# The 32nd largest score of a row, found from the larger and the smaller ones of key pairs

## The chip, the core and the metric

The kernel runs on one core of one Trainium2 chip. A core has five engines with instruction queues of their own: PE (TensorE, matrix products and transposes), DVE (VectorE), ACT (ScalarE), POOL (GpSimd) and SP (SyncE, which here only issues DMAs). They work side by side and meet at semaphores. SBUF is the working memory of 128 partitions, PSUM holds what PE writes. The metric is the device time of one execution in microseconds; less is better. A profiled execution records every instruction on that core.

## The reference

Eight batches of eight heads; each head has 576 queries and 576 keys of 64 numbers. For each query the 32 highest scores are kept, the rest is masked, and the softmax of what is left weighs the values. The result goes through a Fourier mixing layer and a two-layer MLP.

```python
scores = scale * np.matmul(q, k.transpose(0, 1, 3, 2))
kth = np.partition(scores, -top_k, axis=-1)[..., -top_k:-top_k + 1]      # top_k = 32
mask = scores >= kth
scores = np.where(mask, scores, -1000000000.0)
scores = scores - np.max(scores, axis=-1, keepdims=True)
attn = np.exp(scores)
attn = attn / (np.sum(attn, axis=-1, keepdims=True) + 1e-09)
attn_out = np.matmul(attn, v)
...
mixed = np.real(fft(fft(x, axis=1), axis=2))                   # x: [8, 576, 512], heads side by side
u = x + mixed
un = (u - mean) / np.sqrt(var + 1e-06)
out = u + np.maximum(un @ w_ch1, 0.0) @ w_ch2                  # 512 -> 2048 -> 512
```

Two numbers per row of scores are needed from the selection: the maximum and the 32nd largest.

## The kernel before

The kernel is one long unrolled program, written out by hand in the order in which each engine gets its instructions. Two heads form a *pair*; 32 pairs make up the eight batches, four to a batch. The 576 queries of a head are cut into four tiles of 128 rows and a tail of 64. A pair has nine *items*: four tiles for each of its two heads (`e` is 0 or 1), and one item that holds the tails of both heads (`e` is `None`). So there are 288 items of 128 rows by 576 scores, 36 to a batch. In the order of a pair, items 0, 1, 2 and 3 are tiles, item 4 is the tails, items 5 to 8 are tiles.

The main loop (from L1589) goes over steps `i`; step `i` issues, among much else:

- on PE the scores of items `i + 3` and `i + 4` if item `i + 3` has `e == 0` (`scores`, L355): two products of 512 keys into two PSUM banks of the pool `ps_s`, which has two, and one product for the last 64 keys ("tails") of both. ACT copies each into an SBUF tile `S` of 576 columns (L425, L396). The 512 keys stand in columns 0 to 511 for `e == 0` with the tails behind them, and in columns 64 to 575 for `e == 1` with the tails in front;
- on DVE the selection (`top_ops`, L428): eight largest of a row (MAX8, L446), strike these out (MATCH_REPLACE8 with a MATCH_VALUE_LOAD, L448), and again; four maxima and three strikes of 576 columns an item. Step `i` has rounds 2 and 3 of item `i` and rounds 0 and 1 of item `i + 1`, interleaved one by one (L1704). Round 0 reads `S` and writes the struck row into a work tile `wk`;
- on POOL `bounds` (L451): the first and the 32nd of the 32 maxima, scaled, into `nt`; later `mask` (L466): ACT forms a penalty from `S` and `nt` (L469), POOL subtracts it (L472);
- on ACT `expo` (L476, its instruction is L480), the exponential of an item a step or two later.

Then the masked weights must be transposed. In the first batch, in pair 7 and in the last pair PE does that (`transposes`, L532). For all others (`by_dma`) ACT copies the two 16-bit halves of each number apart into `wk` (`plane`, L487), SP writes them to DRAM (L506) and reads them back transposed two or more steps later (`turn`, L515). `wk` is then free for another item; there are three such tiles for pairs of items and one for tails. PE multiplies the transposed weights by the values (`attend`, L576), in the first batch in pieces in the step behind the item, later four or five steps behind it.

The Fourier mixing and the MLP of a batch run in the steps of the next batch: PE's work for them is cut into units that a planner by expected PE costs (`fixed_cost`, `level`) spreads evenly over the steps, and which are put between the steps' other PE work. Since the last batch has no next one, its MLP runs alone at the end. In the first batch the MLP's weights are converted instead, on ACT, POOL and DVE (L209 to L238), and `centre` subtracts means from them.

Each engine takes its instructions in order, so one that waits holds all behind it.

Of the kernel before, what the change touches and what calls it, by code (L numbers as in the profile page):

```python
# [16 lines left out]
TOPK = 32  # L17
# [69 lines left out]
def kernel(  # L87
# [9 lines left out]
    nc = tc.nc  # L97
    B, H, S, D = q.shape
# [21 lines left out]

    fs_np, fd_np, sg_np, turn_np, rows_np = _tables(S, DM)
    fs_d = nc.inline_tensor(fs_np, name="c_fs")
    fd_d = nc.inline_tensor(fd_np, name="c_fd")
    sg_d = nc.inline_tensor(sg_np, name="c_sg")
    turn_d = nc.inline_tensor(turn_np, name="c_turn")
    rows_d = nc.inline_tensor(rows_np, name="c_rows")
# [116 lines left out]
    nat, qT_of, kT_of, v_of, PT, Ssb, Wk, Wp, M8, Nt = ({} for _ in range(10))  # L243
# [111 lines left out]
    def scores(i, part):  # L355
# [26 lines left out]
        if part == 1:  # L382

            copy = nc.scalar.copy if i else nc.vector.tensor_copy
            shape, name = [P, NF * P], f"sp_{i}_t"
            if by_dma(i):
                sp = ps_t.tile(shape, F32, name=name, tag="tp")
            else:
                sp = ps_s.tile(shape, F32, name=name, tag="sp") if i else bank(shape, name)

            q_end = P * t + rows
            nc.tensor.matmul(  # L392
                sp[:, 0:P], lhsT=qT[:, q_end - P:q_end], rhs=kt_t, start=True, stop=True
            )
            for h, (s_t, r, _, tails) in enumerate(to):
                copy(out=s_t[r, tails], in_=sp[P - rows:P, TAIL * h:TAIL * (h + 1)])  # L396
            return 0.3
# [21 lines left out]
        for h, (s_t, r, keys, _) in enumerate(to):  # L419
            hd = slice(D * h, D * (h + 1))  # L420
            sp = ps_s.tile([P, NF * P], F32, name=f"sp_{i}_{h}", tag="sp")
            nc.tensor.matmul(  # L422
# [5 lines left out]
    def top_ops(i, rounds):  # L428

        if not 0 <= i < N:  # L430
            return []
        if i not in Wk:
            e = items[i][2]
            if e != 1:

                if e is None:
                    Wp[i] = attp.tile([P, 1, S], F32, name=f"wk_{i}", tag="W1", bufs=1)
                else:
                    Wp[i] = attp.tile([P, 2, S], F32, name=f"wk_{i}", tag="W", bufs=3)
            Wk[i] = Wp[i - 1][:, 1, :] if e == 1 else Wp[i][:, 0, :]  # L440
            M8[i] = small.tile([P, TOPK], F32, name=f"m8_{i}", tag="m8", bufs=5)
        w, m, s = Wk[i], M8[i], Ssb[i]
        ops = []
        for r in rounds:
            src, m8 = s if r == 0 else w, m[:, 8 * r:8 * r + 8]
            ops.append(lambda src=src, m8=m8: nc.vector.max(out=m8, in_=src))  # L446
            if r < TOPK // 8 - 1:
                ops.append(lambda src=src, m8=m8: nc.vector.match_replace(w, m8, src, NEG))  # L448
        return ops

    def bounds(i):  # L451

        if i < N:
            Nt[i] = small.tile([P, 2], F32, name=f"nt_{i}", tag="nt", bufs=6)
            nc.gpsimd.tensor_tensor(  # L455
                out=Nt[i], in0=M8.pop(i)[:, 0:TOPK:TOPK - 1], in1=cc, op=ALU.mult
            )

# [901 lines left out]
    nc.vector.memset(cc[:, 0:1], -1.0)  # L1360

# [30 lines left out]
    prep("q", 0, ((2, NF), (NF, NC)))  # L1392
    scores(2, 0)
# [192 lines left out]
    for op in top_ops(0, (0, 1)):  # L1586
        op()
    i, carry = 0, 0.0
    while i < N + 5 or plan or queue or sums:  # L1589
        now[0] = i  # L1590
        run(i, "begin")
# [112 lines left out]
        first, second = top_ops(i, (2, 3)), top_ops(i + 1, (0, 1))  # L1704
        for n in range(max(len(first), len(second))):
            for ops in (second, first):
                if n < len(ops):
                    ops[n]()
                if ops is first and n == len(first) - 1:
                    run(i, "shift")  # L1710
        if not first:
# [4 lines left out]
        some_sums(max(2.1 - planned, 0.0))  # L1716
        bounds(i)
# [50 lines left out]
```

## Time and profile before

| what | value |
|---|---|
| median of three runs | 1781.06 us (1779.12 to 1782.7) |
| profiled execution, its time | 1780.27 us |
| its span, first to last instruction | 1778.5 us |
| mean granted TensorE clock | 0.964 |
| PE, DVE, ACT, POOL busy | 92%, 87%, 72%, 51% of the span |
| selection on DVE: MAX8 of `wk`, MAX8 of `S` | 617.4 us in 864, 214.5 us in 288 |
| selection on DVE: MATCH_REPLACE8 of `wk`, of `S` | 424.8 us in 576, 212.5 us in 288 |
| mask on POOL (L472) | 407.6 us in 288 |
| bounds on POOL (L455) | 58.7 us in 288, the last at 1603.5 us |

The span leaves out what lies before the first and behind the last instruction, 1.8 us of the profiled execution's own time. Busy time is the union of an engine's instructions. A line of a group names engine, operation, output and input with their shapes, the number of instructions, their busy time in us, the mean length of one in ns, and the idle time just before them with what ended it. A line of the order of time starts with the start and the length in us. Instructions of one engine can overlap by a little in these records, so the distance from one start to the next tells better what one costs than its length does. The page's chain of work that ended last goes through PE for 48% of the span, DVE 16%, ACT 16%, POOL 14%.

### The profile page before, as it was taken

What the parts mean: (1) busy time and instruction counts of PE and PEld (TensorE: products, weight loads), DVE (VectorE), ACT (ScalarE), POOL (GpSimd) and SP (SyncE); (2) the same over time, 40 slices, a digit from 0 to 9 for tenths busy, and PEclk for the clock granted to TensorE, in tenths of its full rate; (3) what the DMA queues carried; (4) which work ended last, traced back from release to release, by engine and by line L of the source; (5) the groups of instructions that cost most, each with busy time, mean ns of one, the idle gap of its engine ahead of it and who ended that gap; (6) DMA issues with size and microseconds to landing.
All of it is one profiled execution on the core that took longest, in us unless ns stands there. A gap on an engine that the chain in (4) does not pass through costs nothing.

```text
span 1778.5 us, 26295 instructions
## 1 busy us (share of the span) xinstructions
PE 1632.1 (92%) x7830; PEld 1040.9 (59%) x7830; DVE 1552.5 (87%) x3319; ACT 1278.8 (72%) x3136; POOL 906.6 (51%) x1268
## 2 busy tenths in 40 slices
PE   5666689999898989999999999999999999999998
PEld 3444455464455755566555755576566755577777
DVE  7999989999999999998999999999999999863121
ACT  6888759887787878876888778877978787653200
POOL 4768846655634565354544665356535564333000
PEclk7778799999999999999999999999999999999999
DMA  5333126651457855586557856595558655643151
GB/s 156 115 102 117 32 81 163 185 152 50 119 145 196 222 131 135 136 233 161 135 136 200 212 133 140 152 240 145 152 132 222 182 135 128 172 114 101 36 180 60
DMA packets 492926, 255.28 MB, mean 144 GB/s; under 512 B 364528, under 2 KB 483056, under 8 KB 492784
## 3 DMA queue, kind: packets, MB, share of 16 engines
q1 hardware_dynamic: 489008, 243.80, 52.5%
q0 software_dynamic: 2816, 9.44, 1.6%
q8 instruction: 63, 1.03, 0.2%
q14 instruction: 79, 0.65, 0.1%
q10 hardware_dynamic: 960, 0.36, 0.1%
HBM read 99.79 MB, written 84.74 MB: 104 GB/s over the span
## 4 chain that ended last, share of the span: by engine, by line
PE 48%; DVE 16%; ACT 16%; POOL 14%; issue 5%; DMA 2%; POOLq 0%; SPq 0%; DVEq 0%; ACTq 0%
PE hp L1055 18%; DVE m L446 7%; DVE wk L448 6%; PE o L585 6%; PE cw L1254 5%; POOL wk L472 5%; PE cv L1254 4%; PE sp L422 4%; ACT wk L469 3%; POOL fold L696 3%; PE cp L1120 2%; ACT wk L493 2%; PE cp L1082 2%; ACT S L425 2%; PE sp_t L392 1%
## 5 line engine op out<-in xcount | busy, mean ns | idle before, releaser
L472 POOL TENSOR_TENSOR wk<-S,wk 128x576 f32<-128x576 f32 x288 | 407.6, 1415 | 418.1 <-ACT wk L469 417.2
L446 DVE MAX8 m<-wk 128x8 f32<-128x576 f32 x864 | 617.4, 741 | 0.1
L1055 PE MATMUL hp<-unT,w 128*128 128x256 f32 (+1 forms) x2048 | 529.6, 409 | 6.8 <-ACT hT L1059 6.0
L1055 PEld LDWEIGHTS hp<-unT,w 128*128 128x128 f32 x2048 | 378.0, 191 | 112.0 <-ACT hT L1059 11.4
L448 DVE MATCH_REPLACE8 wk<-m,wk 128x576 f32<-128x576 f32 x576 | 424.8, 737 | 0.0
L469 ACT ACTIVATE wk<-S,nt 128x576 f32<-128x576 f32 x288 | 224.3, 779 | 96.8 <-POOL nt L455 96.3
L493 ACT COPY wk<-S 128x576 uint16<-128x576 uint16 x468 | 290.2, 673 | 0.0
L446 DVE MAX8 m<-S 128x8 f32<-128x576 f32 x288 | 214.5, 745 | 11.6 <-ACT S L396 11.6
L480 ACT ACTIVATE S<-wk,nt 128x576 f32<-128x576 f32 x234 | 185.1, 791 | 46.7 <-POOL wk L472 45.4
L448 DVE MATCH_REPLACE8 wk<-m,S 128x576 f32<-128x576 f32 x288 | 212.5, 738 | 0.0
L1082 PE MATMUL cp<-w,hT 128*128 128x512 f32 x448 | 206.0, 598 | 0.0
L1059 ACT ACTIVATE hT<-hp 128x320 f32<-128x320 f32 (+1 forms) x256 | 104.1, 411 | 140.7 <-PE hp L1055 139.7
L585 PE MATMUL o<-PT,v 128*64 128x256 f32 (+3 forms) x1440 | 196.1, 417 | 5.6 <-DVE wk L448 2.1
L422 PE MATMUL sp<-kT,qT 64*128 64x512 f32 (+1 forms) x528 | 160.1, 668 | 6.7 <-ACT S L414 3.6
L585 PEld LDWEIGHTS o<-PT,v 128*64 128x64 f32 x1440 | 113.2, 154 | 84.1 <-issue 24.8
L425 ACT COPY S<-sp 128x512 f32<-128x512 f32 (+1 forms) x264 | 141.7, 589 | 26.2 <-PE sp L422 25.2
L455 POOL TENSOR_TENSOR nt<-m,cc 128x2 f32<-128x2 f32 x288 | 58.7, 204 | 166.9 <-DVE m L446 160.4
L1254 PE MATMUL cw<-w,hT 128*128 128x256 f32 x512 | 119.7, 383 | 9.1 <-ACT ct L1225 6.2
L1082 PEld LDWEIGHTS cp<-w,hT 128*128 128x128 f32 x448 | 81.3, 193 | 75.1 <-issue 74.7
L392 PEld LDWEIGHTS sp_t<-kt,qT 128*128 128x128 f32 x320 | 51.7, 195 | 111.4 <-issue 73.3
L1254 PEld LDWEIGHTS cw<-w,hT 128*128 128x128 f32 x512 | 94.5, 190 | 27.3 <-ACT ct L1225 8.4
L1254 PE MATMUL cv<-w,hT 128*128 128x256 f32 x432 | 100.4, 383 | 6.6 <-DMA w<-w_parts 2.8
(155 smaller groups left out, 2036.3 us busy)
## 6 DMA issues: line engine op xcount, KB each, us to landing
planes<-wk SPq DMA_DIRECT2D x208, 288.0 KB, 2.7
w<-w_parts SPq DMA_DIRECT2D x94, 512.0 KB, 4.7
space<-in_moe_w_ch_dram SPq DMA_DIRECT2D x32, 512.0 KB, 3.6
nat<-in_q_dram SPq DMA_DIRECT2D x128, 64.0 KB, 2.3
v<-in_v_dram SPq DMA_DIRECT2D x32, 256.0 KB, 3.4
nat<-in_k_dram SPq DMA_DIRECT2D x62, 128.0 KB, 2.8
planes<-wk SPq DMA_DIRECT2D x52, 144.0 KB, 2.7
w_parts<-w_t POOLq DMA_DIRECT2D x8, 512.0 KB, 4.0
```

Source lines behind the costliest of these rows:

```text
L422: nc.tensor.matmul(sp[r], lhsT=qT[hd, q_cols], rhs=kT[hd, :], start=True, stop=True)
L425: nc.scalar.copy(out=s_t[r, keys], in_=sp[r])
L446: ops.append(lambda src=src, m8=m8: nc.vector.max(out=m8, in_=src))
L448: ops.append(lambda src=src, m8=m8: nc.vector.match_replace(w, m8, src, NEG))
L469: nc.scalar.activation(out=w, in_=Ssb[i], func=AF.Relu, scale=-FAR, bias=Nt[i][:, 1:2])
L472: nc.gpsimd.tensor_tensor(out=w, in0=Ssb[i], in1=w, op=ALU.subtract)
L480: nc.scalar.activation(out=Ssb[i] if by_dma(i) else w, in_=w, func=AF.Exp, bias=Nt.pop(i)[:, 0:1], accum_out=den_t[pair % 3][:, c:c + 1],)
L493: nc.scalar.copy(out=words[:, half, :], in_=src[:, half, :])
L585: nc.tensor.matmul(o[D * e:D * (e + 1), c0:c1], lhsT=vv[:, e, c, :], rhs=pt[:, NF if c == NF else (NF + 1) * e + c, c0:c1], start=(c == 0) ...
L1055: nc.tensor.matmul(hp[:, 0:w], lhsT=w1[:, dt, P * it:P * (it + 1)], rhs=unT[:, dt, 0:w], start=(dt == 0), stop=(dt == NDT - 1),)
L1082: nc.tensor.matmul(cp, lhsT=hT[:, it, P * n:P * (n + 1)], rhs=w2[:, it, :], start=(it == 0), stop=(it == NIT - 1),)
L1254: nc.tensor.matmul(dst, lhsT=h()[a][:, kc, :], rhs=rhs_of(kc), start=start and kc == 0, stop=kc == NK - 1, skip_group_check=True,)
```

## The change

The 256 items that are tiles become *paired*; the 32 tails items keep the old way.

For a paired item the 512 keys are halved: score `j` of the first half and score `j` of the second form a pair. `split` takes the larger of each pair into `wk` columns 0 to 255 and the smaller into columns 320 to 575, two DVE instructions of 256 columns, which read the second half from PSUM (`sp_of` keeps the bank) and the first half from its copy in `S`. `tails_along` copies the item's 64 tail scores into columns 256 to 319 on POOL. The selection then runs over the first 320 columns, four maxima and three strikes. The maxima of ranks 1 to 8 are kept, those of ranks 9 to 24 are written over, ranks 25 to 32 are kept; the eight largest of the 256 smaller ones stand beside them, and a last maximum over these 16 numbers gives eight, the last of which is the 32nd largest of all. That holds if fewer than eight smaller ones are among the row's 32 largest. `bounds` therefore also forms the difference between this number and the eighth of the smaller ones (POOL, one column, four columns in turn), DVE keeps the least of these twice in each pair of heads (`least_over`), and near the end PE adds up the rows with a difference of zero or less (`count_rows`). All engines load that count after the whole computation, and if it is over zero they run a second, complete copy of the program, `forward(..., False)`, with the old selection.

The order changes with it. `split` and `tails_along` of an item with `e == 0` stand at the head of step `i` for item `i + 2`, while the first maximum of that item still stands in step `i + 1`. `split` of an item with `e == 1` stands behind the fourth selection instruction of step `i` for item `i + 3`. The score banks are held until the splits have read them. The three `wk` tiles are named in turn by hand. The tail scores of both heads go into the transposes' banks (`ps_t`) after the first batch, and into a bank of `ps_m` in it. The constant tables are made outside the two calls of `forward`.

```diff
+    found = pool.tile([P, 8], F32, name="found", tag="found")
+    over, again = found[:, 0:NOVER + 1], found[0:1, 7:8].bitcast(I32)
+    args = (tc, q, k, v, moe_w_ch1, moe_w_ch2, out, tables, over, again)
+    forward(*args, True)
+    rows = nc.values_load(again, min_val=0, max_val=P)
+    with tc.If(rows > 0):
+        forward(*args, False)
...
-            if by_dma(i):
+            if i >= PER_BATCH:
                 sp = ps_t.tile(shape, F32, name=name, tag="tp")
             else:
-                sp = ps_s.tile(shape, F32, name=name, tag="sp") if i else bank(shape, name)
+                sp = bank(shape, name)
...
+            if e is not None:
+                sp_of[i + h] = sp, keys
...
+    w_ring = [attp.tile([P, 2, S], F32, name=f"w_{n}", tag=f"ring{n}", bufs=1) for n in range(3)]
+    HALF = NF * P // 2
+    WON = HALF + TAIL
...
+    def split(i):
+
+        if not paired(i):
+            return
+        w, (sp, keys) = work(i), sp_of.pop(i)
+        near_half = Ssb[i][:, keys][:, 0:HALF]
+        for to, op in ((w[:, 0:HALF], ALU.max), (w[:, WON:S], ALU.min)):
+            nc.vector.tensor_tensor(out=to, in0=sp[:, HALF:2 * HALF], in1=near_half, op=op)
+
+    def tails_along(i):
+
+        if paired(i):
+            e = items[i][2]
+            tails = slice(0, TAIL) if e else slice(NF * P, S)
+            nc.gpsimd.tensor_copy(out=work(i)[:, HALF:WON], in_=Ssb[i][:, tails])
+
+    def top_ops(i, part):
...
+        won = w[:, 0:WON] if pairs else w
+
+        place = (0, 1, 1, 2) if pairs else (0, 1, 2, 3)
+
+        def best(r):
+            n, src = place[r], won if r or pairs else s
+            return lambda: nc.vector.max(out=m[:, 8 * n:8 * n + 8], in_=src)
+
+        def strike(r):
+            n, src = place[r], won if r or pairs else s
+            return lambda: nc.vector.match_replace(won, m[:, 8 * n:8 * n + 8], src, NEG)
+
+        if part == 0:
+            return [best(0), strike(0), best(1), strike(1)]
+        ops = [best(2), strike(2), best(3)]
+        if pairs:
+            ops.insert(0, lambda: nc.vector.max(out=m[:, 24:32], in_=w[:, WON:S]))
+            ops.append(lambda: nc.vector.max(out=m[:, 8:16], in_=m[:, 16:32]))
         return ops
...
+            if pairs:
+                r = i % PER_PAIR
+                n = (r - (r > 4)) % NOVER
+                nc.gpsimd.tensor_tensor(
+                    out=over[:, n:n + 1], in0=m[:, 15:16], in1=m[:, 31:32], op=ALU.subtract
+                )
+
+    def least_over():
+        nc.vector.tensor_reduce(
+            out=over[:, NOVER:], in_=over, op=ALU.min, axis=mybir.AxisListType.X
+        )
...
+    def count_rows():
+
+        got = bank([1, 1], "rows")
+        nc.tensor.matmul(got, lhsT=over[:, NOVER:], rhs=cc[:, 0:1], start=True, stop=True)
+        nc.vector.tensor_scalar(
+            out=again, in0=got, scalar1=-1.0, scalar2=None, op0=ALU.mult
+        )
+        return 0.2
+
+    if in_pairs:
+        for n in range(NPAIR):
+            at(PER_PAIR * n + NOVER, "least", least_over)
+            at(PER_PAIR * (n + 1), "least", least_over)
...
+        at(N + 4, "pe", count_rows)
...
         now[0] = i
+        if i + 2 < N and items[i + 2][2] == 0:
+            split(i + 2)
+        if i + 2 < N and by_dma(i + 2):
+            tails_along(i + 2)
...
-        first, second = top_ops(i, (2, 3)), top_ops(i + 1, (0, 1))
+        if i + 2 < N and not by_dma(i + 2):
+            tails_along(i + 2)
+        first, second = top_ops(i, 1), top_ops(i + 1, 0)
         for n in range(max(len(first), len(second))):
...
+            if n == 1 and i + 3 < N and items[i + 3][2] == 1:
+                split(i + 3)
```

## The prediction

> **What bounds the kernel now.** I read the page's busy times first, then the windows by stage, then the groups by form, and last the order of time in a steady step and in a step of the first batch. The busy shares say that two engines are nearly full.
>
> ```profile
> PE 1632.1 (92%) x7830; PEld 1040.9 (59%) x7830; DVE 1552.5 (87%) x3319; ACT 1278.8 (72%) x3136; POOL 906.6 (51%) x1268
> ```
>
> An average hides which of them ends last where, so the same by stage (length; then busy us and instructions of PE, weight loads, DVE, ACT, POOL; granted clock; DMA share; GB/s):
>
> ```profile
> 0.00:240.00 240.00, 155.70 (x765) 96.32 (x767) 228.68 (x485) 185.50 (x440) 166.75 (x178) 0.77 0.32 98
> 250.00:800.00 550.00, 514.13 (x2402) 308.42 (x2402) 532.83 (x1138) 438.92 (x1084) 304.75 (x436) 0.98 0.60 156
> 800.00:1550.00 750.00, 735.38 (x3545) 458.14 (x3549) 706.08 (x1512) 590.32 (x1443) 392.88 (x584) 1.00 0.65 163
> 1550.00:1778.00 228.00, 218.01 (x1057) 171.61 (x1052) 78.99 (x172) 58.13 (x153) 42.02 (x70) 1.00 0.34 101
> ```
>
> The reader is to see three regimes. In the first batch and its hand-over (its 36th bounds instruction stands at 215.2) DVE is full (95%, and 99% from 50 to 200) while PE has 84 us of holes. From 800 on PE is 98% busy and DVE 94%: PE has only 14.6 us of holes in 750. At the end PE works alone. From 250 to 800 PE has 35.9 us of holes. Is a busy PE at its rate? Matmul ends are modelled, so I read starts:
>
> ```profile
> 1133.71 6.63 PE L1055 MATMUL hp<-unT,w 128*128 128x320 f32 x24
> ```
>
> That is 0.276 us for each matmul, though its group's mean duration is 433 ns. Adding the start-to-start times of all groups of one batch (1122.68 to 1316.14, 193.5 us) gives about 189 us. So PE is truly full there, and no relief of DVE can give more than its holes.
>
> What DVE does, by form, and a stretch of DVE alone in order of time:
>
> ```profile
> L446 DVE MAX8 m<-wk 128x8 f32<-128x576 f32 x864 | 617.4, 741 | 0.1
> L448 DVE MATCH_REPLACE8 wk<-m,wk 128x576 f32<-128x576 f32 x576 | 424.8, 737 | 0.0
> ...
> L630 DVE TENSOR_TENSOR x<-tpx,rd 128x256 f32<-128x256 f32 x57 | 24.0, 421 | 49.9 <-PE tpx L626 42.1 <-DMA out_dram<-x,out_list 5.4 <-PE hp L1055 1.0
> ```
>
> ```profile
> 1130.60 0.74 DVE L446 MAX8 m<-S 128x8 f32<-128x576 f32 x1
> 1131.27 0.73 DVE L446 MAX8 m<-wk 128x8 f32<-128x576 f32 x1
> ...
> 1135.42 0.41 DVE L630 TENSOR_TENSOR x<-tpx,rd 128x256 f32<-128x256 f32 x1
> 1135.75 0.74 DVE L446 MAX8 m<-S 128x8 f32<-128x576 f32 x1
> ```
>
> A pass over 576 columns occupies DVE for 0.67 us start to start, not 0.74, and the seven passes of an item with their three value loads take 4.82 us (1130.60 to 1135.42). A 128x256 tensor_tensor with its input in PSUM takes 0.33.
>
> **DVE, per paired item.** 256 of the 288 items become paired. Removed: 4.82 us. Added: seven passes over 320 columns. The slope per column comes from the adds at L880: 690 ns at 512 columns, 415 at 256, 1.07 ns a column; 0.67 less 256 columns is 0.40, so 2.77 us. Bounds: 0.37 (in proportion to width) and 0.67 (a pass does not shrink). The maximum of the 256 smaller ones by the same slope: 0.33. Three value loads: 0.18. The two splits are L630's form: 0.33 each, 0.66 (0.27, the 64x128 form's duration, to 0.42, its full duration). The last maximum of 16 numbers: 0.16, nearest to the reciprocal of 4 columns (161 ns); 0.06 to 0.25, since it directly follows the maximum it reads. Sum 4.10, saving 0.72 an item: 184 us. The 64 small minima cost 0.17 each (the 5-column tensor_scalar, 172 ns), 11 us. Net 173 us of DVE's 1552, or 0.6 us a step over nine items. With each pass at 0.67 DVE would instead do 1.2 us more an item; the two tensor_tensor rows and the smaller batch-norm rows all shrink with width, so I give that end little weight.
>
> [...]
>
> **What of this reaches the end, by stage.**
>
> First batch. It takes 5.55 us a step (27 bounds instructions at L455 between 50 and 200). Per step DVE is busy 5.51, ACT 4.75, POOL 4.43. DVE falls to about 4.9. POOL gains a 128x64 copy (0.25, between the 128x4 copy's 190 ns and the 64x64 add's 314) and a one-column subtraction (0.19, the 5-column rows): 0.39 a step, to 4.82. So three engines meet at 4.8 to 4.9, and the most to gain is 36 steps of 0.64, 23 us. But a loop comes in between:
>
> ```profile
> 107.57 2.72 PE L585 MATMUL o<-PT,v 128*64 128x128 f32 x20
> ...
> 110.22 1.13 PE L422 MATMUL sp<-kT,qT 64*128 64x512 f32 x4
> ...
> 111.38 1.07 ACT L425 COPY S<-sp 128x512 f32<-128x512 f32 x2
> ...
> 111.99 0.74 DVE L446 MAX8 m<-S 128x8 f32<-128x576 f32 x1
> ```
>
> PE's scores stand behind the attend matmuls, which wait for the previous item's exp. The split needs these scores at the head of a DVE step one step sooner than the first maximum did: here the first copy ends at 111.9 and DVE's step starts at 111.99. The slack is nothing. From the end of the DVE step whose exp the attend needs, to the copy, is two steps, 11 us, plus 0.2 for the subtraction that now stands between bounds and mask on POOL. Attend precedes paired scores so in two places of each nine steps, which ties four steps of nine to 11.2 us a pair. The other five can fall by 0.5: 20 steps, 10 us, less eight times 0.2. I take -8 (bounds -23 and +8, the second if all steps are tied, rival 2).
>
> 250 to 1550. DVE gets 10% of slack and PE stays. PE's 50 us of holes are waits on ACT above all (transposes behind L396 7.1 us, xT 3.3, unT 3.3 and kT 2.6 between 250 and 800). ACT is late where bounds on POOL wait for DVE, so part goes. I take 15, three tenths (0 to 50; next late is ACT's own order). Behind a split that waits stand both items' maxima, and behind those bounds and mask, which nobody needs for four steps here. The splits hold the two score banks until the middle of the next DVE step; PE needs them two PE steps later, so this is hidden while DVE is no more than 3 us behind. The tail scores move to the transposes' banks in the two later pairs that don't go by DMA, and to a bank of their own in the first batch: 10 instructions of 0.2 us each, nothing. SP gets no new DMA. POOL's tails copy now stands ahead of the mask and the fold work and waits for ACT's copy of the tails, emitted one step earlier, and for the ring's buffer: in one pair of items of each nine, its previous planes transfer (1142.67 plus 2.7 to landing) lands at 1145.4, as the DVE step starts at 1145.39. It is covered by POOL's 45% of idle time; if ACT is later, DVE and POOL stand there (rival 2).
>
> 1550 to the end. Two us earlier at most for the last items; -2. The last 122 us, from 1656, are PE alone and stay.
>
> The end. Five engines load the count, compare and jump over the second forward. No row shows a load of a register or a jump. Below: 0, beside the 2.6 us landing of the last output, which each run waits for anyway. Above: two small transfers in sequence at 4.4 us, some 9, and I take +5, the middle. [...]
>
> Sum: 1780.27 - 8 - 15 - 2 + 5 = 1760. The profiled execution is 0.8 below the median of the three runs, 1781.06, so the two agree within 0.05%.
>
> **Rivals.** 1: PE's holes were all DVE's doing and the first batch reaches its floor: -23, -50, -2, +5, so 1710. For it: PE's share of the chain of waits is only 48%, DVE, ACT and POOL taking turns. Against: the holes are behind ACT.
>
> 2, slower: the early split becomes the bound. Place: the head of DVE's step and POOL's tails copy. In the first batch every pair of steps then costs the loop plus 0.45 us of new POOL work, 18 times, +8; per nine steps afterwards one stand of up to 2 us on the planes transfer that also holds masks and folds, 26 of them with a fifth on PE's path, +10; end +5 to +9. About 1805, and 1793 with half of it. It decides once the loop is longer than 11.1 us for two steps. For it: zero slack at 111.99 and 1145.39. Against: DVE has 1.2 us to lose in two steps before it is where it was.
>
> 3: the gain is off the path everywhere: first batch -3, middle -3, end +5: 1779, the same.
>
> 4: a row fails and everything runs again, about 3540. From the reference's inputs I counted how many of the smaller of each pair are among a row's 32 largest: 5 at most in all rows, and eight would be needed. Under 1 in 100.
>
> **How the numbers follow.** A measurement of this kernel tells 0.2% from nothing. Chances: the forecast 0.54 (its own range 1745 to 1772), rival 1 0.14, rival 3 0.08, rival 2 0.23, rival 4 0.01. Faster 0.69, same 0.08, slower 0.23. The range 1725 to 1793 leaves out the far half of rivals 1 and 2.
>
> **What would show it.** Passes of 0.40 us start to start; splits of 0.42 duration without long waits before them; DVE busy near 1380; the 36th bounds instruction near 207 rather than 215.2; PE idle from 250 to the end of attention about 35; the last bounds near 1580 rather than at 1603.5; under 9 us between the last DMA issue's landing and the end. I am wrong if DVE waits on S or on planes for more than 100 us in all, if passes do not shrink, or if PE's holes stay at 50.

## The result, and the profile after

The changed kernel takes 1796.06 us (1795.84 to 1798.32) against 1780.09 (1777.33 to 1782.7) for the kernel before, each the median of four runs: a ratio of 1.0093, 95% interval 1.0075 to 1.0111, so 0.9% slower. The forecast was 1760. The second, complete program never runs. The profiled execution takes 1795.85 us, its span is 1794.0, the mean granted clock 0.968 (0.964 before).

The page's busy times of the changed kernel:

```profile
PE 1637.0 (91%) x7832; PEld 1040.3 (58%) x7832; DVE 1387.2 (77%) x4410; ACT 1280.8 (71%) x3136; POOL 993.6 (55%) x1780
```

DVE lost 165 us of work, as planned, and the kernel became slower. The same by stage (stretch, length, then busy us and instructions of PE, weight loads, DVE, ACT, POOL; granted clock, DMA share, GB/s):

```profile
0.00:240.00 240.00, 152.81 (x772) 93.32 (x773) 205.54 (x631) 186.06 (x441) 176.62 (x248) 0.81 0.34 98
250.00:800.00 550.00, 510.64 (x2371) 304.26 (x2370) 467.26 (x1512) 434.60 (x1074) 331.12 (x613) 0.98 0.60 152
800.00:1550.00 750.00, 734.88 (x3520) 456.28 (x3519) 626.73 (x2033) 590.59 (x1440) 435.95 (x825) 1.00 0.63 161
```

PE's holes, which were to be filled, are 39.4 us from 250 to 800 (35.9 before) and 15.1 from 800 to 1550 (14.6). In the same 550 us PE issued 31 matmuls fewer, and 25 fewer in the 750. Where that builds up is seen from the bounds instructions on POOL, of which both kernels have one per item. Their starts in us:

| bounds instruction | before | after | difference |
|---|---|---|---|
| 36 | 226.6 | 225.5 | -1.1 |
| 72 | 419.1 | 424.0 | +4.9 |
| 144 | 807.1 | 819.0 | +11.9 |
| 216 | 1199.7 | 1210.4 | +10.7 |
| 287, the last | 1603.5 | 1615.9 | +12.4 |
| from the last one to the end of the span | 175.0 | 178.1 | +3.1 |

(They are counted from 0. The prediction's 36th bounds instruction is number 35 here: it starts at 214.6, 215.2 before, and 207 was forecast.) So the first batch gains one microsecond, the time to 1600 loses 13.5 and the end 3.

The DVE groups of the changed kernel by form (busy us, mean ns of one, idle time before them and what ended it):

```profile
L498 DVE MAX8 m<-w 128x8 f32<-128x320 f32 x1024 | 482.5, 482 | 28.4 <-POOL w L481 27.4
L502 DVE MATCH_REPLACE8 w<-m,w 128x320 f32<-128x320 f32 x768 | 361.6, 475 | 0.0
L474 DVE TENSOR_TENSOR w<-sp,S 128x256 f32<-128x256 f32 x512 | 189.9, 412 | 117.4 <-ACT S L444 85.0 <-DMA planes<-w 26.0 <-ACT ct L1299 5.0
```

The work costs what it was to cost. What is new is the right-hand column: 117 us in which DVE stands before a split, 85 of them until ACT has copied the scores. Who waits for DVE then? ACT's waits for the bounds, in the view of waits (us in total, times, longest), first of the kernel before, then of the changed one:

```profile
ACT wk L469 <- POOL nt L455: 96.3, 78, 4.8
```

```profile
ACT w L543 <- POOL nt L518: 111.8, 82, 5.2
```

DVE has 165 us less to do, and the engine that waits for its bounds waits longer. One such event of the changed kernel in order of time (start, length, engine; the idle time just before stands in brackets):

```profile
673.82 1.89 PE L441 MATMUL sp<-kT,qT 64*128 64x512 f32 x4 [0.58 <-ACT S L431]
...
675.66 0.19 DVE L686 RECIPROCAL rd<-rd 128x6 f32<-128x6 f32 x1 [0.53 <-ACT rd L685]
...
677.52 0.77 ACT L554 ACTIVATE S<-w,nt 128x576 f32<-128x576 f32 x1
...
678.29 0.76 ACT L543 ACTIVATE w<-S,nt 128x576 f32<-128x576 f32 x1
678.96 1.23 ACT L567 COPY w<-S 128x576 uint16<-128x576 uint16 x2
680.21 1.07 ACT L444 COPY S<-sp 128x512 f32<-128x512 f32 x2
...
680.83 0.75 DVE L474 TENSOR_TENSOR w<-sp,S 128x256 f32<-128x256 f32 x2 [4.98 <-ACT S L444]
...
686.89 0.19 POOL L518 TENSOR_TENSOR nt<-m,cc 128x2 f32<-128x2 f32 x1 [2.45 <-DVE m L509]
...
687.11 0.78 ACT L543 ACTIVATE w<-S,nt 128x576 f32<-128x576 f32 x1 [0.97 <-POOL nt L518]
```

PE has the scores at 675.7. ACT, which works in its order, has among other things an exponential, a penalty and two 16-bit copies ahead of them, and copies the scores at 680.21. DVE stands for 4.98 us, because a split heads its step. Behind that split is the rest of the selection of the item whose bounds come next: POOL waits 2.45 us for them, ACT 0.97 us for POOL, and what follows in ACT's order is late, the next copy of scores too.

What it takes from PE is small each time. The matmuls have the same order in both traces up to 1640 us, so each can be set against its counterpart. The delay grows in steps of 0.4 to 3.2 us, at the transposes of the tail queries, the scores, the first MLP product, one second MLP product. Late in the run the same three steps come back every batch of 193 us, 0.6, 0.4 and 1.1 us. The third of them, once in each kernel (before, then after):

```profile
1107.44 1.13 PE L422 MATMUL sp<-kT,qT 64*128 64x512 f32 x4
```

```profile
1112.83 1.52 ACT L431 COPY S<-sp 64x256 f32<-64x256 f32 x4
...
1113.64 1.89 PE L441 MATMUL sp<-kT,qT 64*128 64x512 f32 x4
```

In the first of these both banks are free and the two heads run side by side: their products start within 0.01 us of each other, and each head's second product 0.53 us after its first. In the other ACT's four copies out of these banks end at 1114.35, after PE has begun, and the second head starts at 1114.41, 0.77 us behind the first. PE counts as busy all the while; the matmul starts show it, the busy share doesn't. Of the 109 such groups after 240 us, nine have their starts spread over more than 1 us, four before the change. In all PE is busy with the score products for 184.5 us, 178.7 before. Not all of that is ACT's doing: in the groups at 278.2 and 703.9 us the second head starts 0.15 us after a split's end, and no copy by ACT has ended for over 2 us. It is only one of the forms that the delay takes: the kernel of run 11 below has eleven such groups, without the loss.

The end: the last output's DMA issue and the end of the span are 1775.29 and 1778.5 before, 1788.02 and 1794.0 after, 2.8 us more, where 5 was predicted.

### The profile page after: what moved, and what is told of

The parts are those of the page before. It is cut to its first block, busy times and chain, and to the rows that moved or that the text cites. A ratio compares the mean times of both kernels' runs of the same rounds, so it can differ in the third digit from the quotient of the medians.

```text
span 1794.0 us, 28106 instructions
## 1 busy us (share of the span) xinstructions
PE 1637.0 (91%) x7832; PEld 1040.3 (58%) x7832; DVE 1387.2 (77%) x4410; ACT 1280.8 (71%) x3136; POOL 993.6 (55%) x1780
## 4 chain that ended last, share of the span: by engine, by line
PE 51%; ACT 20%; POOL 13%; DVE 10%; issue 5%; DMA 0%; SPq 0%; POOLq 0%; DVEq 0%; ACTq 0%
PE hp L1129 20%; PE cw L1328 6%; PE o L659 5%; PE cv L1328 5%; PE sp L441 4%; POOL w L546 4%; ACT w L543 3%; DVE m L498 3%; ACT w L567 3%; PE cp L1194 3%; POOL fold L770 2%; ACT S L444 2%; DVE w L502 2%; PE cp L1156 2%; DVE w L474 1%
## 5 line engine op out<-in xcount | busy, mean ns | idle before, releaser
L546 POOL TENSOR_TENSOR w<-S,w 128x576 f32<-128x576 f32 x256 | 364.4, 1423 | 308.9 <-ACT w L543 308.6
L498 DVE MAX8 m<-w 128x8 f32<-128x320 f32 x1024 | 482.5, 482 | 28.4 <-POOL w L481 27.4
L1129 PEld LDWEIGHTS hp<-unT,w 128*128 128x128 f32 x2048 | 378.1, 191 | 115.9 <-ACT hT L1133 13.5
L502 DVE MATCH_REPLACE8 w<-m,w 128x320 f32<-128x320 f32 x768 | 361.6, 475 | 0.0
L474 DVE TENSOR_TENSOR w<-sp,S 128x256 f32<-128x256 f32 x512 | 189.9, 412 | 117.4 <-ACT S L444 85.0
L543 ACT ACTIVATE w<-S,nt 128x576 f32<-128x576 f32 x256 | 198.9, 777 | 112.3 <-POOL nt L518 111.8
L567 ACT COPY w<-S 128x576 uint16<-128x576 uint16 x416 | 257.8, 672 | 0.0
L554 ACT ACTIVATE S<-w,nt 128x576 f32<-128x576 f32 x208 | 164.8, 792 | 48.5 <-POOL w L546 47.6
L441 PE MATMUL sp<-kT,qT 64*128 64x512 f32 (+1 forms) x528 | 166.0, 665 | 10.8 <-ACT kT L356 3.5
L508 DVE MAX8 m<-w 128x8 f32<-128x256 f32 x256 | 104.5, 408 | 0.0
```

Of the source, the lines that this page charges most:

```text
L441: nc.tensor.matmul(sp[r], lhsT=qT[hd, q_cols], rhs=kT[hd, :], start=True, stop=True)
L474: nc.vector.tensor_tensor(out=to, in0=sp[:, HALF:2 * HALF], in1=near_half, op=op)
L498: return lambda: nc.vector.max(out=m[:, 8 * n:8 * n + 8], in_=src)
L502: return lambda: nc.vector.match_replace(won, m[:, 8 * n:8 * n + 8], src, NEG)
L543: nc.scalar.activation(out=w, in_=Ssb[i], func=AF.Relu, scale=-FAR, bias=Nt[i][:, 1:2])
L546: nc.gpsimd.tensor_tensor(out=w, in0=Ssb[i], in1=w, op=ALU.subtract)
```

## The experiments

Ratios are to the kernel before, run on the same chip in the same job; in brackets the 95% interval. Kernels whose edit is given against the changed kernel keep all else of it.

**1. How much is relief of DVE worth at all?** The kernel before, with the passes of tile items over 320 columns. This leaves 256 keys of each of these rows out of the selection.

```diff
-            src, m8 = s if r == 0 else w, m[:, 8 * r:8 * r + 8]
+            n = S if items[i][2] is None else NF * P // 2 + TAIL
+            src, m8 = (s if r == 0 else w)[:, 0:n], m[:, 8 * r:8 * r + 8]
```

> The kernel before, with the four maxima and three strikes of every tile item run over the first 320 of its 576 columns. It leaves 256 keys out of the selection, so the output differs; nothing else is changed, no split, no POOL work, no check. DVE is relieved by 7 x 0.27 = 1.9 us an item, 480 us in all. Theory A (PE's own work and ACT's order hold the time, DVE was busy beside them): 1773 to 1782, PE holes from 250 to 1550 still 40 to 50 us, the 36th bounds instruction not before 212. Rival B (DVE did hold PE, and the early split of the change gave the gain back): 1755 or less, holes under 30 us, the 36th bounds instruction near 200.

1760.5 us, 0.9897 (0.988 to 0.9913). DVE's busy time falls to 1100.6 us (63%), ACT's wait for bounds from 96.3 to 69.7 us, PE's holes to 30.8 and 12.4 us, 43.2 in place of 50.5. The time lies between the two ranges that were expected. With 1.9 us an item taken from DVE (seven passes of 0.40 us in place of 0.67), two and a half times as much as the change takes, the kernel gains 18 us, and the 36th bounds instruction starts at 211.2 in place of 215.2. So PE's holes were DVE's doing only in small part, and the first batch is not held by DVE alone.

**2. The splits one step later,** behind ACT's copies, from `S` alone, with the tails' copy behind the bounds.

```diff
-            nc.vector.tensor_tensor(out=to, in0=sp[:, HALF:2 * HALF], in1=near_half, op=op)
+            nc.vector.tensor_tensor(out=to, in0=far_half, in1=near_half, op=op)
...
-        if i + 2 < N and items[i + 2][2] == 0:
-            split(i + 2)
+        if 1 < i + 1 < N:
+            split(i + 1)
```

> The changed kernel with both splits one step later (head of the step that has the item's first maximum), both inputs from SBUF so that the score banks are free as before, and the copy of the tails behind the bounds on POOL. Same work on every engine. If the early place of the split and of the tails copy cost the 12.7 us that PE lost (theory B's second half): 1780 to 1785, DVE's waits on S and on planes under 30 us instead of 85 and 26. If POOL's added work or PE's fullness did it: 1793 to 1798.

1839.29 us, 1.0333 (1.0314 to 1.0352). This is far above both ranges. The wait for `S` is gone, and something else came (groups of DVE and POOL by form):

```profile
L474 DVE TENSOR_TENSOR w<-S 128x256 f32<-128x256 f32 x512 | 271.0, 569 | 0.5 <-ACT S L554 0.3 <-ACT hT L1133 0.2
...
L518 POOL TENSOR_TENSOR nt<-m,cc 128x2 f32<-128x2 f32 x288 | 78.5, 273 | 214.8 <-DVE m L509 164.3 <-DVE found L529 21.4 <-DVE m L498 16.8
```

With both inputs in SBUF a split takes 569 ns in the mean, not 412, and POOL's bounds of two columns 273, not 195. Single instructions of the kernel before show the like. A 128x256 tensor_tensor on DVE with both inputs in SBUF (L685) took 1.12 us at 225.76, while POOL ran two of the same shape and its bounds, and 0.43 at 1627.32, while POOL ran nothing. Those bounds of POOL, at 226.57, took 0.36 us, against 0.20 in the mean, and a DVE instruction with an input in PSUM (L630, at 225.31) took 0.42 beside POOL. The slower rows of this run agree with that, on both engines. DVE also waits 123.4 us (171 times) for POOL's tails copy. The run shows that the place can't be had by this form of split; it decides nothing on the place itself.

**3. Without the count of rows:** no difference, no least, no count, no load, no second program.

```diff
-    rows = nc.values_load(again, min_val=0, max_val=P)
-    with tc.If(rows > 0):
-        forward(*args, False)
...
-                nc.gpsimd.tensor_tensor(
-                    out=over[:, n:n + 1], in0=m[:, 15:16], in1=m[:, 31:32], op=ALU.subtract
-                )
```

> The changed kernel without the row check: no difference on POOL, no least, no count, no load of the count and no second forward. The selection stays. If the check costs only its end: 1793, that is 3 us less. If the subtraction between bounds and mask on POOL (0.19 us, 256 times) is what makes ACT and PE late: 1787 or less.

1791.87 us, 1.0078 (1.0061 to 1.0095). All of it costs 4 us by the medians, 2.7 by the ratios, and the two intervals overlap. From the last bounds to the end it is 175.0 us, as before the change, so the 3 us there come of the count, its load and the jump. DVE's wait for `S` stays (84.6 us), ACT's for the bounds too (110.3).

**4. POOL relieved:** bounds, difference and tails' copy on DVE.

```diff
-            nc.gpsimd.tensor_copy(out=work(i)[:, HALF:WON], in_=Ssb[i][:, tails])
+            nc.vector.tensor_copy(out=work(i)[:, HALF:WON], in_=Ssb[i][:, tails])
...
-            nc.gpsimd.tensor_tensor(
+            nc.vector.tensor_tensor(
                 out=Nt[i], in0=m[:, 0:last + 1:last], in1=cc, op=ALU.mult
```

> The changed kernel with POOL's small instructions moved to DVE: the bounds, the difference and the copy of the tails. POOL falls by 170 us, DVE rises by some 110 of the 173 that it had gained. If POOL's queue is what makes the exp late and with it ACT and PE: 1785 or less. If the early place of the split is the cause: 1794 or more, since the copy then stands at the head of DVE's step as well.

1867.72 us, 1.0494 (1.0474 to 1.0513), the slowest of all. POOL's relief brings nothing in this form, since DVE pays more than POOL did; what POOL's queue costs by itself the run can't tell:

```profile
L481 DVE COPY w<-S 128x64 f32<-128x64 f32 x256 | 88.1, 344 | 65.8 <-ACT S L413 65.8
L518 DVE TENSOR_TENSOR nt<-m,cc 128x2 f32<-128x2 f32 x288 | 85.0, 295 | 7.9
```

The copy takes 344 ns on DVE against 250 on POOL, the bounds 295 against 195, and there is a second instruction at which DVE stands for ACT.

**5 and 6. The change taken apart,** both without the count of rows. Splits without the tails' copy (the tails take no part in the selection), and tails' copy without splits (the selection runs over the first 320 columns of `S`, the maximum of 256 over the first 256, so the other keys are left out).

```diff
-            nc.gpsimd.tensor_copy(out=work(i)[:, HALF:WON], in_=Ssb[i][:, tails])
+            work(i)
```

> The changed kernel without the row check and without POOL's copy of the tails: the 64 tail scores of a head are left out of the selection (the passes run over the 256 larger and 64 of the smaller ones, so the DVE work is the same). The splits stand where the change has them, early and from PSUM. Measured so far: DVE relieved alone 1760.5, the change without its check 1791.9, 31 us apart. If the early split is what costs them: 1785 to 1792. If POOL's tails copy, with the waits at the head of POOL's and DVE's steps, costs them: 1762 to 1770.

```diff
+        return
         w, (sp, keys) = work(i), sp_of.pop(i)
...
-            nc.gpsimd.tensor_copy(out=work(i)[:, HALF:WON], in_=Ssb[i][:, tails])
+            nc.gpsimd.tensor_copy(out=work(i)[:, WON:WON + TAIL], in_=Ssb[i][:, tails])
```

> The changed kernel without the row check and without the two splits; the first maximum and strike read 320 columns of S, and POOL copies the tails at the change's early place into columns that nobody reads. It leaves 256 keys out of the selection and DVE has 0.66 us an item less to do than in the change. If the early split costs the 31 us: 1762 to 1768. If POOL's copy at its early place costs them (it holds mask and bounds behind it): 1780 or more.

Splits alone: 1787.88 us, 1.0053 (1.0035 to 1.007), slower, and ACT's wait for the bounds is 112.9 us. Tails alone: 1767.86, 0.9944 (0.9921 to 0.9967), faster, that wait 67.8 us. Both are in the range for the splits as the cost: the loss is in them. POOL's copy is small: 4 us between the kernels of runs 3 and 5, whose intervals overlap. Whether a split costs by its length or by its wait these two don't tell.

**7. All splits at the end of the DVE step,** the first head's a whole step later, the second's half a step; the tails' copy behind the penalty.

```diff
-        if i + 2 < N and items[i + 2][2] == 0:
-            split(i + 2)
...
+        if i + 2 < N and items[i + 2][2] == 0:
+            split(i + 2)
+            split(i + 3)
```

> The whole changed kernel, check included, with both splits of a pair of items at the end of the DVE step at whose head and middle they stood, still from PSUM, and the tails copy behind the mask on POOL instead of ahead of it (outside the first batch's way of working). If it is the early place that makes DVE stand: 1770 to 1785, DVE's wait for S at the split under 30 us instead of 85. If the length of the work and not its place costs: 1793 to 1800.

1802.81 us, 1.0143 (1.0121 to 1.0164). DVE no longer waits for `S`. It waits for POOL, and now PE waits for DVE (waits of DVE, then of PE):

```profile
DVE m L498 <- POOL w L481: 112.0, 74, 6.1
...
PE sp L441 <- DVE w L474: 17.5, 14, 4.8
...
PE sp L424 <- DVE w L474: 7.5, 4, 2.1
```

The wait for `S` went as expected and the time didn't. A late split holds the two score banks: PE waits 25 us for them (2.7 in the changed kernel), and it is busy with the score products for 193.9 us (184.5 there, 178.7 before the change). ACT's wait for bounds falls to 73.1 us without any use. The tails' copy moved along with the splits, so the run bounds the place from the other side and no more.

**8 and 9. The wait by itself.** No split, no tails' copy, no count of rows; two maxima over 256 columns stand where the splits stood, for the same DVE time. In one kernel they read a constant, in the other the score bank and its copy. Neither's result is used, and the selection leaves 256 keys out.

```diff
-        for to, op in ((w[:, 0:HALF], ALU.max), (w[:, WON:S], ALU.min)):
-            nc.vector.tensor_tensor(out=to, in0=sp[:, HALF:2 * HALF], in1=near_half, op=op)
+        for n in range(2):
+            nc.vector.max(out=over, in_=turns.rearrange("p a c -> p (a c)")[:, 0:HALF])
```

> The changed kernel without the check and without POOL's tails copy, and with the two splits replaced, at the very same places in DVE's order, by two maxima over 256 columns of a constant tile: DVE works as long as before, but waits for nothing there and holds no bank and no ring buffer. The selection reads 320 columns of S (256 keys are left out). With real splits this was 1787.9. If the splits cost by what they wait for: 1762 to 1770. If they cost by their length, since any DVE work delays the bounds: 1780 or more.

```diff
-            nc.vector.tensor_tensor(out=to, in0=sp[:, HALF:2 * HALF], in1=near_half, op=op)
+        for src in (sp[:, HALF:2 * HALF], Ssb[i][:, keys][:, 0:HALF]):
+            nc.vector.max(out=over, in_=src)
```

> The same, with the two maxima reading what the splits read, the second half in PSUM and the first half in S, but writing eight columns that nobody needs: the wait for S and the hold on the score banks are back, the wait for the ring buffer's planes transfer is not. If S and the banks carry the cost: 1782 to 1788. If the ring buffer does: 1766 to 1772.

1774.16 us, 0.9974 (0.9962 to 0.9986), and 1797.15, 1.0103 (1.0078 to 1.0128). DVE groups by form, first with the constant, then with the scores:

```profile
L470 DVE MAX8 found<-turns 128x8 f32<-128x256 f32 x512 | 214.6, 419 | 8.9
```

```profile
L470 DVE MAX8 found<-S 128x8 f32<-128x256 f32 x256 | 109.6, 428 | 8.8
L470 DVE MAX8 found<-sp 128x8 f32<-128x256 f32 x256 | 107.4, 419 | 88.2 <-ACT S L441 87.5
```

The first lies between its two ranges, the second 9 us above the higher one; the order of the two is as expected if the waits cost. The same work at the same place costs 23 us more when it reads the scores just made. These maxima write nothing into the work tiles, so the tiles' buffers have no part in it. ACT's wait for the bounds is 85.4 us in the one and 112.1 in the other. The page names ACT's copy as what ends the wait even of the maximum that reads only the bank. But the maxima also hold the score banks longer. What PE loses to that directly is small: it waits 3.2 us for these maxima, all of it in the first 240 us, and after that the second head's products start right behind one of them (0.05 us) in two groups, 2 us later than with both banks free. The loss comes later: bounds instruction 36 starts at 226.3 with the constant and at 226.6 with the scores, the last at 1596.4 and 1619.2. So this pair settles the cause: nearly all of what costs is that DVE's queue stands at its head for ACT.

**10. From `S` alone and late, but in pairs over all 576 columns,** 288 and 288, so that no tails' copy is needed; the splits at the head of the step that has the first maximum.

```diff
-    WON = HALF + TAIL
+    WON = S // 2
...
+            nc.vector.tensor_tensor(out=to, in0=s[:, WON:S], in1=s[:, 0:WON], op=op)
```

> The whole changed kernel, check included, with all 576 columns of S halved into 288 pairs at the head of the step that has the item's first maximum, both inputs from SBUF: no early wait, no bank held, no tails copy on POOL. The splits were 0.57 us each against POOL's use of the same memory (0.37 from PSUM), so DVE is relieved by some 0.4 us an item only. If the waits of the early split are the cost and not DVE's length: 1775 to 1785. If DVE's length is: 1790 or more.

1791.72 us, 1.0075 (1.0053 to 1.0096). 12 us of waits for `S`, no POOL copy, but a split with two SBUF inputs takes 646 ns for 288 columns, and DVE's busy time is 1458 us. By what was expected this falls to DVE's length and against the waits. The longer splits may have taken back what the place saves, but POOL's bounds are slower here too (274 ns) and DVE is no busier than 1458 us where 1552 gave 1778: the run doesn't separate them, and its reason stays open.

**11. Only the place, by half a step:** both splits from PSUM and `S` as in the change, each one behind the fourth and the eighth selection instruction of the DVE step.

```diff
-        if i + 2 < N and items[i + 2][2] == 0:
-            split(i + 2)
...
             if n == 1 and i + 3 < N and items[i + 3][2] == 1:
+                split(i + 2)
+            if n == 3 and i + 3 < N and items[i + 3][2] == 1:
                 split(i + 3)
```

> The whole changed kernel with the two splits of a pair moved by half a step, to behind the fourth and the eighth selection instruction, the tails copy left where it is. At the old place DVE waited 85 us for S, at the end of the step PE waited 25 us for the banks. If there is room between them: 1785 to 1792; if the two waits meet: 1795 to 1800.

1778.64 us, 1.0004 (0.9994 to 1.0013): as fast as the kernel before, and 16 us better than the change by the ratios. DVE's waits:

```profile
DVE m L498 <- POOL w L481: 65.2, 46, 5.2
DVE w L474 <- DMA planes<-w: 23.1, 7, 4.6
```

The wait for `S` is 16.2 us (85.0 in the change). ACT waits 82.7 us for the bounds, PE has 30.3 and 12.4 us of holes, close to what narrow passes gave in run 1. The whole change is in this kernel, the count of rows too. It is better than either range that was expected.

But the banks now cost. One group of score products of this kernel in order of time, with the splits between its two heads:

```profile
533.57 1.12 PE L441 MATMUL sp<-kT,qT 64*128 64x512 f32 x2
...
534.76 0.73 DVE L474 TENSOR_TENSOR w<-sp,S 128x256 f32<-128x256 f32 x2
...
535.63 1.09 PE L441 MATMUL sp<-kT,qT 64*128 64x512 f32 x2 [0.95 <-DVE m L509]
```

The second head starts 0.15 us after the splits' end, 2.07 us behind the first, and less than half of that counts as idle time. In nine of the 109 groups after 240 us it starts right behind a split (0.05 to 0.15 us), which adds 11 us in all. So PE's idle time is 134.3 us of the span, 146.3 before the change, but PE is busy with the score products for 190.7 us, 178.7 before. Half a step trades one wait for the other.

**12 and 13. What still holds it.** Of the 65 us for POOL's tails copy: that copy on DVE, as a reduction over one element, first behind the splits, then right ahead of the first maximum that reads it.

```diff
-            nc.gpsimd.tensor_copy(out=work(i)[:, HALF:WON], in_=Ssb[i][:, tails])
+            nc.vector.tensor_reduce(
+                out=work(i)[:, HALF:WON],
+                in_=Ssb[i][:, tails].rearrange("p (t one) -> p t one", one=1),
+                op=ALU.max, axis=mybir.AxisListType.X,
+            )
...
                 split(i + 2)
+                tails_along(i + 2)
...
                 split(i + 3)
+                tails_along(i + 3)
```

> The whole change with the splits half a step later, as in the run before (1778.64 us against 1777.76 of the kernel before), and one thing more: the copy of the 64 tails into the working tile goes from POOL to DVE, which does it as a reduction over one element ahead of the maximum that reads them. In the run before DVE waited 65 us for that copy on POOL, and the kernel with the tails' copy alone was about 7 us above the one with no copy at all. If that wait, on DVE's way to the bounds, is what keeps the moved split from a gain, it goes: 1768 to 1775 us, DVE's wait for POOL's copy gone, its busy time up by 256 copies of 0.1 to 0.3 us (25 to 80 us). The rival: DVE's own time for the copies costs as much as the wait that they replace, since they stand in the same place on the way to the bounds: 1779 to 1800 us, with ACT's wait for the bounds at 83 us or more.

```diff
         def best(r):
             n, src = place[r], won if r or pairs else s
-            return lambda: nc.vector.max(out=m[:, 8 * n:8 * n + 8], in_=src)
+
+            def go():
+                if r == 0:
+                    tails_along(i)
+                nc.vector.max(out=m[:, 8 * n:8 * n + 8], in_=src)
+            return go
```

> The whole change with the splits half a step later, and the copy of the 64 tails on DVE, right ahead of the first maximum that reads them, a step after the place of the last run; the tails have long been in SBUF by then. In the last run the copy on DVE took 0.13 us start to start, so 256 of them are about 35 us of DVE, in place of the 65 us that it waited for POOL's copies. If that run's loss (1803.93 us) came of the copy's place, where it waited 52 us for ACT's copy of the other scores, and not of the engine, this one comes to 1768 to 1779 us. The rival: any instruction more on DVE's way to the bounds costs what it takes, whoever else is relieved: 1785 us or more.

Behind the splits: 1803.93 us, 1.0137 (1.0119 to 1.0154). Ahead of the first maximum: 1782.8, 1.0019 (1.001 to 1.0028). The same 256 instructions, a step apart, in the DVE groups by form:

```profile
L481 DVE TENSOR_REDUCE w<-S 128x64 f32<-128x64 f32 x256 | 53.1, 207 | 52.4 <-ACT S L413 52.4
```

```profile
L481 DVE TENSOR_REDUCE w<-S 128x64 f32<-128x64 f32 x256 | 52.5, 205 | 4.1 <-ACT S L413 4.1
```

52 us of standing for ACT in the one, 4 in the other, and 21 us between the two kernels. ACT waits 104.8 us for the bounds in the first and 90.4 in the second. Most of the difference arises in the first batch: bounds instruction 36 starts at 243.5 in run 12 and at 224.5 in run 13. That DVE's queue stands early for ACT is the mistake of the change once more, and the expectation of run 12 made it by looking at POOL alone. But run 12 also holds the banks longer (score products 201.2 us of PE's busy time against 191.3), so the copies' place isn't the one cause. Run 12 is 4 us above its rival's range, and run 13 falls between its two. With the copy on DVE in the late place the kernel is 0.15% slower than run 11, not faster: moving the copy brings nothing. As DVE then pays for the copy itself, that doesn't tell what the wait for POOL costs. No kernel that computes the whole result beat the kernel before.

## Why the prediction was wrong

**The sum in one line.** Between the kernels of runs 8, 5 and 3 and the change, each adds one thing to the last: the relief of DVE without the waits 0.9974 (-4.6 us; DVE busy 1407 us there), the splits themselves in place of two maxima on a constant 1.0053 (+14.1), the tails' copy 1.0078 (+4.5), the count of rows 1.0093 (+2.7). Each ratio is uncertain by about 0.0016, some 3 us, so the last two steps are hardly clear of noise. In run 8 the first maximum reads `S`, in run 5 a work tile that the splits have written, so that step isn't the wait alone. The forecast had -25, nothing, nothing, +5.

**DVE per item: right.** Passes over 320 columns start 0.40 us apart, two splits 0.65. DVE is busy 1387 us, 1380 was forecast. The measured row of 0.33 us for a 128x256 tensor_tensor with its input in PSUM held for the splits.

**First batch, -8: mis-sized.** It gave 1.1. Narrow passes that relieve DVE by 1.9 us an item gave only 5 there (run 1). That DVE was full for 150 us did not mean that it was what the step lasted for. The loop over PE's scores and ACT's copies, which the prediction itself wrote down with a slack of nothing, would explain it; no run took it apart.

**250 to 1550, -15: the step that failed.** It came to +13.5. Part of it is size: the relief alone, with no new wait, is worth 4.6 us in the whole kernel, and three tenths of PE's holes were not to be had for 0.7 us an item when the 1.9 us of run 1 took 7.3 of the 50.5. The larger part is one sentence of the prediction, that behind a waiting split stand both items' selection, bounds and penalty, "which nobody needs for four steps here". The product with the values needs them in four or five steps. ACT needs them now: its penalty for the item comes in the next stretch of its order, and all copies for PE stand behind that. A queue's patience is that of the next instruction behind it, not of the item's last reader. The condition written down for being wrong, over 100 us of waits on `S` or planes, was met with 111, and so was the one on PE's holes, which stayed at 54.5.

**Holding the score banks costs nothing: nearly right in the change** (2.7 us of waits, and some of the 5.8 us by which PE is longer busy with the score products). It is wrong half a step later (12 us more of that busy time than before, run 11) and at the end of the step (25 us of waits and 15 more of busy time, run 7). The splits' place has two sides, and the change stood on the early one.

**POOL's copy and the difference: nothing, mis-sized.** The durations were right (250 and 190 ns for 0.25 and 0.19), the copy cost about 4 us (runs 5 and 3), and that its place in POOL's queue is the reason wasn't shown.

**The end, -2 and +5: right in size.** It gave +3 behind the last bounds, and the two us ahead of that didn't come.

**The rivals.** Rival 2, the early split as the bound, gave 1793 to 1805, which is where it came out, with a chance of 0.23. Its place was right, the head of DVE's step; its terms were not. The first batch lost nothing, where it had +8. Its second term hung on the planes transfer, which holds DVE for 26 us in the change; the wait for `S`, 85 us, which the prediction had shown as a loop in the first batch only, goes on all through the run. Rival 3 had the size of the relief nearly right (-6 in all, against -4.6), and none of the waits. One slip of a hundredth: by the chances of the forecast and the rivals, faster is 0.68 and slower 0.24, not 0.69 and 0.23.

**What stays open.** Why two maxima on the scores cost more (run 9, 1.0103) than real splits there (run 5, 1.0053). Why run 10 gains nothing. And whether run 11 can reach run 8's gain: in the profiled executions its last bounds come 6.1 us earlier than before the change, run 8's 7.0, and the end then takes 3 us of it back; by its median nothing is left. Against run 8 its PE is idle for 9 us less and busy for 12.7 longer, 12 of these in the score products, so the held banks are the first to ask about. A third score bank wasn't tried, nor were both inputs of a split in PSUM or a fourth work tile.

## What to carry to other kernels

When an instruction is moved ahead in an engine's queue, look at what its inputs wait for and then at who needs the *next* instruction behind it: some 145 us less work on DVE were worth 5 us here, and real splits, which wait at the head of its steps, cost 14. Look also at who needs what it holds meanwhile, and not by idle time alone: PE counted as busy while it stood between two products. Measure the wait alone by putting an instruction of the same length there that reads a constant, and try places half a step apart before giving up on an idea; the same change moved by half a step was 16 us faster. A full engine is not a bound until a run with much less work on it shows a gain.

## What the runs showed of the hardware

- A 128x256 tensor_tensor on DVE with one input in PSUM took 409 to 413 ns in the mean in all kernels that have it, with both in SBUF 569 in the mean, with POOL's two-column bounds going from 195 to 273 ns.
- 128x64 from SBUF to SBUF took 344 ns on DVE as a copy (run 4) and 207 and 205 as a reduction over one element (runs 12 and 13); the three kernels differ in place as well.
- Loading a count into five engines and jumping over a second complete program took 2.8 us at the end: 5.98 us from the last output's DMA issue to the end of the span, 3.21 before.
- A pair of score products that found its second bank still being read took 1.89 us (at 1113.64 in the changed kernel), not 1.13, at full "busy" of PE.
